# Two 96-point transforms rewritten from split products to plain fp32 strips of 32 columns

## The chip, the cores and the metric

The kernel runs on one core of one Trainium2 chip. The metric is the device time of one execution in microseconds (us); the runs shown are three executions, and their median is the time before.

## What is computed

The reference chains three layers on 24,576 rows of 256 numbers. First a Fourier layer: a real FFT over 3072 positions, a complex 256 by 256 mixing with bias, soft shrinkage by 0.01, and the inverse FFT.

```
X = np.fft.rfft(x, axis=1)
Yr = Xr @ w_r - Xi @ w_i + b_r
Yi = Xr @ w_i + Xi @ w_r + b_i
...
y = np.fft.irfft(Y, n=x.shape[1], axis=1)
```

Then every row picks one of 8 experts by `argmax(x @ w_gate)`; an expert takes at most 768 rows, in order, and applies `relu(h @ w1) @ w2` times the gate's probability. Last comes a second MLP with `h * softmax(h)` and a layer norm between its two products. Experts fill up early, so the kernel transforms only the first three sequences of the batch (`FIRST = 3`) and checks that this was enough.

## The kernel before, in words

The FFT of 3072 positions is done in two steps, 3072 = 96 x 32. Per sequence (a "turn" b = 0, 1, 2):

- **Forward, first step** (`forward`, L949): a 96-point transform of 16 pieces, each 96 x 512 numbers. `prepare` (L332) splits a piece into a high and a low fp32r part (`split`, L280: a copy on ACT, L281, and a subtraction on DVE, L282), and `dft` (L311) makes three fp32r matmuls of them (L314 to L316). Four pieces of sixteen (`WHOLE`; three in the first turn, `WHOLE_0`) skip the split and run as one plain fp32 matmul (L325), which the trace shows as two records. Two pieces share one PSUM tile of 96 x 1024; `leave` (L341) moves it to SBUF on ACT or DVE, `park` (L357) writes it to DRAM (`gdram`, L359), eight writes per turn.
- **Units** (`units`, L985): twelve units u read the data back turned round (`relay`, L366), make 32-point transforms (`stage2`, L380), split them (L383, L384), mix (`mix`, L413), shrink (DVE, L419 to L422) and go back (`inv1`, L430).
- **Tail** (`tail`, L1001): gate logits (L440, four strips of 32 columns beside each other, plain fp32, 384 columns wide), then per piece n four transposes (L459), a split of the transposed piece (L281, L282), the 96-point inverse (`inv2`, L465, again `dft`, `psy`), a move to a `yt` buffer (L473, four of them in turn) and a write to `ydram` (L474). The routing steps `local` and `place` (L504 to L518) stand between the pieces; the marks that follow (L533, L534 on DVE, L536 on POOL, L542 on PE) run in the next turn's units.

After the third turn come the expert blocks (from 338 us to the end), which the change leaves alone.

All loads and writes of these stages are issued by one queue, SP, in program order, and its transfers take eight semaphore lanes in turn: a ninth waits for the first to land. The Tile scheduler sets the order on each engine, so that work without dependencies, like the zeroing of the output (`out`, L909, 512 KB each) and loads of expert weights (L595, L598), is put where it finds room. `load_x` (L296) loads the next sequence in eight parts q: five before the turn ends, q = 5 to 7 inside `forward`, as buffers come free:

```
def x_at(q, roomy):
    if roomy and q >= 3:
        return v3(o_ht + 1024 * (q - 3), 4, D, N1)
    return v3(o_yt + 1024 * (q - 3) if q in (3, 4) else o_xr + 1024 * (q % 5), 4, D, N1)
```

Of the kernel before, what the change touches and what calls it, by code (L numbers as in the profile page):

```python
# [8 lines left out]
F32 = mybir.dt.float32  # L9
# [19 lines left out]
AHEAD = 4  # L29
LEAVE_0 = (1, 3, 5)  # L30
LEAVE = (1, 3, 5)
GATHER = 9


# [9 lines left out]
NCH = 8  # L44
COUNT = 3
SUMS = 7
YT = (13, 15)
LOOK = 4
LOG = 0
WARM = 4  # L50
KEEP = 8
STEPS = (3, 3, 2)
ZEROS = ((0, 0, 0, 0), (2, 2, 2, 2), (2, 2, 2, 2))
WHOLE = (2, 5, 8, 11)
WHOLE_0 = (0, 1, 14)
PERSIST = 16472
EARLY = (0, 1)

# [71 lines left out]
def _body(tc, x, w_r, w_i, b_r, b_i, w_gate, w1, w2, w_in, w_out, g_ln, cap, con, out):  # L130
# [15 lines left out]
    with sp as sb, dp as dr, pp as ps:  # L146
# [49 lines left out]
        o_lt = o_rt  # L196
        ident = v(o_id, 128)
        fraw = v3(o_f, 2, N1, N1)
        o_fs = region(384)
        renew(o_fs)  # L200
        f_h, f_l = R(v3(o_fs, 2, N1, N1)), R(v3(o_fs + 192, 2, N1, N1))
        bias, bias0 = v(o_b, 256), v(o_b0, 256)
        zero = v(o_zero, 128)
        wg = v3(o_wg, 2, 32)
# [21 lines left out]
        g3 = lambda: v3(o_g, N2, D, N1)  # L226
# [38 lines left out]

        def load_f():
            dma(out=fraw, in_=con["c_f"])
            act(f_h, fraw, ACTF.Copy)
            vec.tensor_tensor(f_l, fraw, f_h.bitcast(F32), ALU.subtract)
# [21 lines left out]
        def x_at(q, roomy):  # L291
            if roomy and q >= 3:
                return v3(o_ht + 1024 * (q - 3), 4, D, N1)
            return v3(o_yt + 1024 * (q - 3) if q in (3, 4) else o_xr + 1024 * (q % 5), 4, D, N1)
# [4 lines left out]
        second_half = [o_tt]  # L299

        def piece(n, roomy=False):
            o = (o_hn, second_half[0])[n // 3 % 2] + 1024 * (n % 3)
            if roomy:
                n %= 10
                if n >= 6:
                    o = o_xb[(n - 6) // 2] + 1024 * (n % 2)
                else:
                    o = (o_hn, second_half[0])[n // 3] + 1024 * (n % 3)
            return R(v(o, 512, N1)), R(v(o + 512, 512, N1))
# [8 lines left out]
        def stage1(q, roomy):  # L318
            p = psum("ps1")
            for j in range(2):  # L320
                n = 2 * q + j
                o, (src, parts) = p[:N1, 512 * j : 512 * j + 512], ready.pop(n)
                gone.add(n)
                if parts is None:
                    mm(o, fraw[:, 0], src, start=True, stop=True)  # L325
                else:
                    dft(o, 0, parts, roomy)
            return p

        ready = {}  # L330

        def prepare(n, roomy):  # L332

            src = x_at(n // 2, roomy).rearrange("p a d -> p (a d)")[:, 512 * (n % 2) : 512 * (n % 2) + 512]
            k = None
            if n not in (WHOLE_0 if roomy else WHOLE):
                k = n - sum(i < n for i in (WHOLE_0 if roomy else WHOLE))
                split(*piece(k, roomy), src)
            ready[n] = src, k

        def leave(q, p, on_vec):  # L341
            dst = v(o_g + 1024 * q, 1024, N1)
            if q == 7:
                act(dst[:, 0:512], p[:N1, 0:512], ACTF.Copy)
                vec.tensor_copy(dst[:, 512:1024], p[:N1, 512:1024])
            elif q in on_vec:
                vec.tensor_copy(dst, p[:N1])
            else:
                act(dst, p[:N1], ACTF.Copy)
            park(q)  # L350

        def gd(g):
            return v((o_ga if g % 12 < 6 else o_gb) + 256 * (g % 6), D)

        turn_of = [0]

        def park(q):  # L357

            dma(out=gdram[turn_of[0] % 2][:, 4 * q : 4 * q + 4, :], in_=g3()[:, 4 * q : 4 * q + 4])  # L359
            if q == 7:  # L360
                turn_of[0] += 1

        def relay(g, n=2):
# [88 lines left out]

        turned, summed = [None, None], [None, None]

        def inv2t(n):
# [9 lines left out]
        def inv2(n, yv):  # L465
            if n % 2 == 0:
                summed[0] = psum("psy")
            p = summed[0][:N1, 512 * (n % 2) : 512 * (n % 2) + 512]
            w = dft(p, 1, n)
            if n % 2:  # L470
                apart(w, summed[1])
            yt = v(o_yt + 512 * (n % 4), 512, N1)
            summed[1] = [vec.tensor_copy(yt, p) if n in YT else act(yt, p, ACTF.Copy)]  # L473
            dma(out=yv[:, 2 * n : 2 * n + 2], in_=yt.rearrange("p (a d) -> p a d", d=D))  # L474


        def route(tok_src, chunk_buffers):
# [468 lines left out]
        def in_order(strict):  # L946
            return pinned() if strict else ExitStack()

        def forward(xb, roomy=False, begun=False):  # L949
            if not begun:  # L950
                begin(roomy)
            last = begun_with.pop()
            for q in range(1, 8):
                for n in range(2 * q + 2, min(2 * q + AHEAD + 2, 16)):
                    if n not in ready and n not in gone:
                        with in_order(roomy):
                            prepare(n, roomy)
                if q + 4 < 8 and not roomy:
                    load_x(xb, q + 4)
                p = stage1(q, roomy)  # L960
                if roomy and q == 7:
                    end = [i for i in nc.cur_bb.bb.instructions if i.engine == mybir.EngineType.PE][-1]
                    with tc.issue_after(end):
                        warm(KEEP)
                with in_order(roomy):
                    leave(q - 1, last, LEAVE_0 if roomy else LEAVE)
                last = p
            with in_order(roomy):
                leave(7, last, ())
            gone.clear()  # L970

        begun_with, gone = [], set()

        def begin(roomy=False):

            for n in range(4):
                with in_order(roomy):
                    prepare(n, roomy)
            begun_with.append(stage1(0, roomy))

        def relays():
# [19 lines left out]
        def tail(yv, steps):  # L1001

            logits(0)
            inv2t(0)
            logits(1)
            for n in range(1, LOOK):
                inv2t(n)
            for n in range(16):
                if n + LOOK < 16:
                    inv2t(n + LOOK)  # L1010
                inv2(n, yv)
                if n == LOG:
                    logits2()
                if n % 2 and n // 2 + 1 in steps:
                    for f in steps[n // 2 + 1]:
                        f()

        csum = bias0
# [151 lines left out]
        for b in range(FIRST):  # L1170
# [25 lines left out]
                    if early:  # L1196
                        early.pop(0)()

            def before_last(last=last, steps=steps):
                while steps:  # L1200
                    steps.pop(0)()
                renew(o_hn)
                if last:
                    renew(o_ga)
                    blocks[0].transposes()
                    sums.extend(column_sums())
                    sums.pop(0)()
                else:
                    begin()

            units(middle, before_last)
            while sums:
                sums.pop(0)()
            renew(o_tt)
            if last:
                renew(o_wi2)
                second_half[0] = o_wi2
            if not last:
                forward(x[b + 1], begun=True)
# [23 lines left out]
        renew(o_hn)  # L1243
        marks.append(all_places)
        run_blocks(blocks, side, slot_b, verdict, marks)

# [65 lines left out]
```

## Time and profile before

| what | value |
|---|---|
| median of three runs | 907.37 us (907.3 to 910.01) |
| the profiled execution, own time | 907.39 us |
| its span, first to last instruction | 905.6 us |
| mean granted TensorE clock | 0.976 |
| PE busy | 858.3 us, 95% |
| DVE busy | 660.2 us, 73% |
| ACT busy | 451.3 us, 50% |
| POOL busy | 302.9 us, 33% |

The 1.8 us between span and own time lie around the instructions. PE is TensorE's matmul, PEld its weight load. In the trace the turns' stages lie at: forward 0 from 5.66 us, units 0 from 32.85, forward 1 from 90.23, tail 0 from 110.34 to 136.62, units 1 after it, forward 2 from 201.43, tail 1 from 215.44 to 244.65, units 2 after it, tail 2 from 314.25 to 338.36. The last `inv1` of a turn (L430, 0.9 us, 91.70 to 92.61 in the first) stands inside the next forward.

### The profile page before, as it was taken

The page shows a single profiled execution, that of the slowest core. Times are in us where ns is not written, and L with a number is a line of the kernel's source. Part 1 is how long each engine was busy: PE and PEld are TensorE (multiplying, and loading weights), DVE is VectorE, ACT ScalarE, POOL GpSimd, SP SyncE. Part 2 cuts the span into 40 slices and gives each one's busy share as a digit, 9 for nine tenths or more (in the row PEclk, how much of TensorE's full clock was granted, in tenths as well). Part 3 has the DMA queues.
Part 4 walks back from the last instruction along what each step waited for, and adds up shares of the span by engine and source line. Part 5 has one row for each costly group of instructions (what it writes and reads, how often), then busy time and mean ns, then how long its engine had stood idle before and what let it go on. Part 6 is the DMA issues. An engine that isn't in the chain of part 4 may idle for free.

```text
span 905.6 us, 15391 instructions
## 1 busy us (share of the span) xinstructions
PE 858.3 (95%) x5585; PEld 763.8 (84%) x5585; DVE 660.2 (73%) x1499; ACT 451.3 (50%) x725; POOL 302.9 (33%) x463
## 2 busy tenths in 40 slices
PE   9599899999899998999999999999999999999993
PEld 5599368995699978989899999899889889999983
DVE  6277579777887687777788778678768768777672
ACT  6254464446734372555466456456446446444450
POOL 0000002200031205363754554454544544445343
PEclk9799899999899998999999999999999999999997
DMA  9989869999541133253465463553564463333220
GB/s 284 303 246 301 275 215 266 309 300 297 195 162 36 36 115 102 70 100 71 103 163 114 123 140 82 117 140 91 108 140 87 112 140 86 73 76 65 53 59 28
DMA packets 206699, 130.90 MB, mean 145 GB/s; under 512 B 122406, under 2 KB 190102, under 8 KB 206486
## 3 DMA queue, kind: packets, MB, share of 16 engines
q1 hardware_dynamic: 201910, 117.20, 49.1%
q0 software_dynamic: 4704, 12.63, 4.4%
q8 instruction: 46, 0.75, 0.3%
q14 instruction: 39, 0.32, 0.1%
HBM read 50.37 MB, written 50.33 MB: 111 GB/s over the span
## 4 chain that ended last, share of the span: by engine, by line
PE 72%; DMA 9%; DVE 7%; issue 6%; POOL 2%; ACT 2%; SPq 0%; POOLq 0%; DVEq 0%; ACTq 0%
PE psH L778 13%; PE pso L893 11%; PE psm L413 8%; PE psY L798 5%; PE psY L797 5%; PE psh L823 4%; PE psh L822 4%; PE psY L795 4%; PE psh L825 4%; DMA r<-r 4%; PE psi L430 3%; PE ps L380 3%; PE psr L542 2%; DVE r L282 1%; DMA r<-moe_w_in 1%
## 5 line engine op out<-in xcount | busy, mean ns | idle before, releaser
L778 PE MATMUL psH<-r,r 128*128 128x384 f32 x768 | 147.7, 340 | 0.5 <-DVE r L282 0.5
L778 PEld LDWEIGHTS psH<-r,r 128*128 128x128 f32 x768 | 135.6, 190 | 2.3 <-DVE r L282 0.8
L893 PE MATMUL pso<-r,r 128*128 128x256 f16 (+1 forms) x792 | 134.6, 274 | 0.5 <-DMA r<-r 0.5
L893 PEld LDWEIGHTS <-r 128*128 128x128 f16 x1080 | 102.2, 98 | 18.8 <-issue 6.9
L413 PE MATMUL psm<-r,r 128*128 128x256 f32 x864 | 112.8, 286 | 2.4 <-DVE r L473 2.2
L536 POOL TENSOR_TENSOR r<-r,r 96x192 f32<-96x192 f32 x24 | 19.3, 822 | 278.9 <-DVE r L392 139.3
L413 PEld LDWEIGHTS psm<-r,r 128*128 128x128 f32 x864 | 106.0, 191 | 2.9 <-ACT r L473 1.4
L781 ACT ACTIVATE r<-psH 128x768 fp32r<-128x768 f32 x64 | 52.0, 813 | 105.8 <-PE psH L778 102.7
L839 DVE SCALAR_TENSOR_TENSOR r<-psh,r 128x1024 f32<-128x1024 f32 x48 | 58.8, 1224 | 51.7 <-ACT r L831 51.7
L282 DVE TENSOR_TENSOR r<-r,r 128x512 fp32r<-128x512 f32 (+2 forms) x115 | 81.4, 722 | 14.3 <-ACT r L281 13.9
L798 PE MATMUL psY<-r,r 128*128 128x384 f32 x256 | 86.5, 338 | 4.6 <-DVE r L782 4.3
L797 PE MATMUL psY<-r,r 128*128 128x384 f32 x256 | 85.7, 335 | 0.0
L831 ACT ACTIVATE r<-psh,r 128x1024 f32<-128x1024 f32 x36 | 43.4, 1205 | 82.9 <-DVE r L830 58.9
L893 PE MATMUL pso<-r 128*128 128x256 f16 x360 | 81.0, 273 | 0.0
L896 POOL DMA_INDIRECT out<-r x48 | 56.0, 1167 | 72.1 <-DVE r L895 65.0
L822 PE MATMUL psh<-r,r 128*128 128x512 f32 x192 | 76.5, 399 | 0.0
L823 PE MATMUL psh<-r,r 128*128 128x512 f32 x192 | 75.6, 394 | 0.0
L281 ACT ACTIVATE r<-r 128x512 fp32r<-128x512 f32 (+2 forms) x115 | 71.4, 647 | 7.5 <-DMA r<-x 6.5
L782 DVE SCALAR_TENSOR_TENSOR r<-psH,r 128x768 fp32r<-128x768 f32 x64 | 61.1, 954 | 12.5 <-ACT r L781 11.3
L732 POOL DMA_INDIRECT r<-ydram,r x48 | 50.6, 1053 | 44.1 <-DVE r L758 14.8
L829 DVE TENSOR_REDUCE r<-psh 128x1 f32<-128x1024 f32 x48 | 58.5, 1218 | 8.6 <-PE psh L825 8.6
L869 POOL TENSOR_SCALAR r<-r 128x1 f32<-128x1 f32 x48 | 12.5, 261 | 146.5 <-ACT r L849 115.3
(192 smaller groups left out, 1803.3 us busy)
## 6 DMA issues: line engine op xcount, KB each, us to landing
out<-r SPq DMA_DIRECT2D x48, 512.0 KB
r<-moe_w SPq DMA_DIRECT2D x32, 512.0 KB
r<-x SPq DMA_DIRECT2D x24, 384.0 KB
gdram<-r SPq DMA_DIRECT2D x24, 384.0 KB
r<-gdram SPq DMA_DIRECT2D x36, 256.0 KB
ydram<-r SPq DMA_DIRECT2D x48, 192.0 KB
r<-moe_w_in SPq DMA_DIRECT2D x4, 512.0 KB
r<-moe_w_out SPq DMA_DIRECT2D x4, 512.0 KB
```

Source lines behind the costliest of these rows:

```text
L281: a = act(hi, src, ACTF.Copy)
L282: return a, eng.tensor_tensor(lo, src, hi.bitcast(F32), ALU.subtract)
L413: mm(p3[:, gi], a, b, start=i == 0, stop=i == len(seq) - 1)
L778: mm(p3[:, fi, 0:BLK], a, b, start=i == 0, stop=i == 5)
L782: vec.scalar_tensor_tensor(hl_, p3[:, :, 0:BLK], 0.0, hh.bitcast(F32), ALU.max, ALU.subtract)
L797: mm(y3[:, d, 0:BLK], a, hh[:, fi], start=False, stop=False)
L798: mm(y3[:, d, 0:BLK], a, hl_[:, fi], start=False, stop=f == 7)
L822: mm(o, a, r, start=k == 0, stop=False)
L823: mm(o, a, w, start=False, stop=False)
L829: vec.tensor_reduce(c(0), p, AX.X, ALU.max, negate=True)
L839: vec.scalar_tensor_tensor(t, p, 1.0, e, ALU.mult, ALU.mult, accum_out=c(3))
L893: mm(p[:, 0:D], a, b, start=n == 0, stop=n == 23)
```

## The change

No piece is split any more. A 96-point transform is computed as three strips of 32 output columns in plain fp32, at column positions 0, 32 and 64 of the array; the fourth position takes a third of another piece. So three PSUM banks hold four pieces: twelve banks per transform where there were sixteen pieces, all 128 partitions full. Bank k holds piece `own(k)` = 1, 2, 3, 5, 6, 7, 9, ... and strip k % 3 of piece 0, 4, 8 or 12.

```diff
-        def dft(o, i, n, roomy=False):
-            hi, lo = piece(n, roomy)
-            return [mm(o, f_h[:, i], hi, start=True, stop=False),
-                    mm(o, f_l[:, i], hi, start=False, stop=False),
-                    mm(o, f_h[:, i], lo, start=False, stop=True)]
+        own = lambda k: 4 * (k // 3) + 1 + k % 3
+        def bank(o, i, k, piece):
+            strips = [(m, piece(own(k))) for m in range(3)] + [(k % 3, piece(4 * (k // 3)))]
+            return [mm(o[32 * j : 32 * j + 32], fraw[:, i, 32 * m : 32 * m + 32], src, start=True, stop=True, tile_position=(0, 32 * j))
+                    for j, (m, src) in enumerate(strips)]
...
-            dma(out=gdram[turn_of[0] % 2][:, 4 * q : 4 * q + 4, :], in_=g3()[:, 4 * q : 4 * q + 4])
+            if t % 3 == 0:
+                dma(out=flat(dram[:, r + 2 : r + 6, :]), in_=src[0:N1])
+                dma(out=thirds(0, r), in_=pairs(src[N1:128]))
+            elif t % 3 == 1:
+                dma(out=dram[:, r + 6 : r + 14, :].rearrange("m (j n) d -> m j (n d)", j=2)[:, :, 0 : 2 * D], in_=pairs(src[0:N1]))
+                dma(out=flat(dram[64:96, r : r + 2, :]), in_=src[N1:128, 0:512])
+                dma(out=flat(dram[0:32, r + 8 : r + 10, :]), in_=src[N1:128, 512:1024])
+            else:
+                dma(out=flat(dram[:, r + 12 : r + 16, :]), in_=src[0:N1])
+                dma(out=thirds(32, r + 8), in_=pairs(src[N1:128]))
...
-            turned[1] = split(*piece(n), p)
+            a = piece(n)
+            turned[1] = [vec.tensor_copy(a, p) if n % 2 else act(a, p, ACTF.Copy)]
...
+            dma(out=yv[:, 2 * own(k) : 2 * own(k) + 2], in_=yt[0:N1].rearrange("p (a d) -> p a d", d=D))
+            dma(out=yv[m : m + 32, r : r + 2], in_=yt[N1:128].rearrange("p (a d) -> p a d", d=D))
...
-                begin(roomy)
+                begin(xb, roomy)
...
+            if not roomy:
+                for q in range(5, 8):
+                    load_x(xb, q)
```

`prepare` is gone. A turn's `leave` moves six tiles of 128 x 1024 where it moved eight of 96 x 1024 (LEAVE is now (1, 3)); `park` makes 14 writes for 8, `inv2` 24 for 16. A transposed piece is moved by one copy, on ACT for even n and on DVE for odd n. The parts q = 5 to 7 of the next sequence get buffers of their own (`o_hn`) and are loaded by `begin`, ahead of the first bank. `place` stands after bank 8 of twelve (turns 0, 1) or bank 7 (turn 2), where it stood after piece 11 or 9 of sixteen. Line numbers shift: L298 is the strips' matmul, L333 to L340 the writes, L361 and L394 were L380 and L413, L365 was L384, L521 and L522 were L533 and L534.

The scheduler's order moves with it. The first place is SP around forward 1 (`x` the next sequence, `out` the zeroing, `gdram` the parked tiles). Before:

```order
L909 DMA out<-r_66 1024x1x128 x8
L297 DMA r_66<-x 96x1024 x3
L909 DMA out<-r_66 1024x1x128 x6
L359 DMA gdram_65<-r_69 96x1024
L297 DMA r_66<-x 96x1024
L359 DMA gdram_65<-r_69 96x1024
L297 DMA r_66<-x 96x1024
L359 DMA gdram_65<-r_69 96x1024 x6
```

Now:

```order
L897 DMA out<-r_66 1024x1x128 x8
L288 DMA r_66<-x 96x1024 x2
L288 DMA r_789<-x 96x1024 x3
L897 DMA out<-r_66 1024x1x128 x4
L332 DMA gdram_65<-r_68 96x1024
L333 DMA gdram_65<-r_68 32x2x512
L335 DMA gdram_65<-r_68 96x2x512
L336 DMA gdram_65<-r_68 32x512
```

The last two parts of x stood behind six zeroing writes and between parked tiles; all of x now stands ahead of four zeroing writes.

The second place is DVE after `place` in tail 0, where units 1 begin (L384 and L365 make the low part that the first mix needs, L473 and L459 move the last results). Before:

```order
L518 CAST r_66<-r_66 96x32
L533 TENSOR_TENSOR r_1222<-r_66 96x512
L473 COPY r_66<-psy 96x512
L384 TENSOR_TENSOR r_71<-ps_1170,r_71 128x4x128
L389 CAST r_71<-r_71 128x256
```

Now:

```order
L506 CAST r_66<-r_66 96x32
L521 TENSOR_TENSOR r_1173<-r_66 96x512
L522 TENSOR_TENSOR r_1173<-r_66 96x192
L521 TENSOR_TENSOR r_66<-r_66 96x512
L522 TENSOR_TENSOR r_66<-r_66 96x192
L522 TENSOR_TENSOR r_1173<-r_66 96x192
L365 TENSOR_TENSOR r_70<-ps_1121,r_70 128x4x128
L370 CAST r_70<-r_70 128x256
L522 TENSOR_TENSOR r_66<-r_66 96x192
L373 TENSOR_SCALAR r_70<-r_70 128x4
```

Five mark steps now stand ahead of L365 where one stood ahead of L384; the third L522 reuses a buffer that POOL has to have read. In turn 1 three stand there.

## Rows read from the trace of the kernel before

**Rows 1.** The page's part 4: the chain that ended last, by engine.
```profile
PE 72%; DMA 9%; DVE 7%; issue 6%; POOL 2%; ACT 2%; SPq 0%; POOLq 0%; DVEq 0%; ACTq 0%
```
**Rows 2.** Waits of PE: line waited for, us in total, times, longest us.
```profile
PE ps L380 <- DMA r<-gdram: 9.7, 1, 9.7
...
PE psr L542 <- POOL r L536: 3.7, 1, 3.7
PE ps L314 <- ACT r L281: 3.4, 2, 1.8
...
PE psy L314 <- ACT r L473: 1.8, 1, 1.8
```
**Rows 3.** Windows by stage: length, busy us by engine, granted clock, DMA share, GB/s.
```profile
90.23:136.62 46.39, 41.66 (x214) 25.07 (x213) 29.20 (x55) 26.22 (x46) 0.00 (x0) 0.93 0.79 247
136.62:147.66 11.04, 9.07 (x73) 8.51 (x71) 9.66 (x27) 5.29 (x12) 2.59 (x4) 1.00 0.89 265
201.43:244.65 43.22, 41.33 (x213) 26.57 (x212) 32.01 (x60) 30.26 (x54) 0.00 (x0) 0.92 0.82 261
244.65:256.54 11.89, 9.08 (x73) 8.54 (x72) 10.88 (x29) 5.16 (x12) 3.12 (x4) 1.00 0.77 255
314.25:338.36 24.11, 24.11 (x162) 16.83 (x162) 19.27 (x44) 16.44 (x32) 0.00 (x0) 1.00 0.33 99
338.36:346.03 7.67, 3.99 (x21) 3.68 (x20) 5.53 (x14) 1.93 (x4) 3.40 (x4) 0.85 0.41 126
```
**Rows 4.** The same view, five microseconds each, in tail 1.
```profile
225.00:230.00 5.00, 5.00 (x34) 3.93 (x32) 4.77 (x12) 5.00 (x11) 0.00 (x0) 1.00 1.00 344
...
235.00:240.00 5.00, 5.00 (x16) 3.44 (x16) 2.31 (x5) 2.94 (x6) 0.00 (x0) 0.50 0.87 273
```
**Rows 5.** Timeline of PE in tail 2: start, us, line, operation, count.
```profile
314.25 1.50 PE L440 MATMUL psl<-r 128*32 128x384 f32 x16
315.68 0.64 PE L459 MATMUL pst<-r 128*96 128x128 f32 x4
316.25 0.83 PE L440 MATMUL psl<-r 128*32 128x384 f32 x2
...
319.00 0.97 PE L459 MATMUL pst<-r 128*96 128x128 f32 x7
319.81 0.60 PE L444 MATMUL psl<-r 128*96 128x128 f32 x4
```
**Rows 6.** Timeline of PE in forward 1.
```profile
97.34 1.02 PE L325 MATMUL ps<-r 96*96 96x512 f32 x2
97.79 0.79 PE L314 MATMUL ps<-r,r 96*96 96x512 f32 x1
98.42 0.39 PE L315 MATMUL ps<-r,r 96*96 96x512 f32 x1
98.65 0.39 PE L316 MATMUL ps<-r,r 96*96 96x512 f32 x1
```
**Rows 7.** Groups by line and form, the strips' weight loads: busy us, mean ns.
```profile
L440 PEld LDWEIGHTS psl<-r 128*32 128x32 f32 x96 | 3.3, 115 | 6.3 <-issue 5.8 <-PE ps L316 0.4
```
**Rows 8.** The same view, the low part of transposed pieces on DVE.
```profile
L282 DVE TENSOR_TENSOR r<-pst,r 96x512 fp32r<-96x512 f32 x48 | 32.2, 681 | 11.4 <-ACT r L281 11.3
```
**Rows 9.** Timeline of SP: issues at the start, and around forward 1.
```profile
15.48 8.18 SPq L359 DMA_DIRECT2D gdram<-r  x8
...
95.94 1.11 SPq L297 DMA_DIRECT2D r<-x  x1
```
**Rows 10.** Timeline of DVE after place in tail 0.
```profile
133.54 0.16 DVE L506 TENSOR_TENSOR r<-pso,r 96x8 f32<-96x8 f32 x1 [0.80 <-PE pso L505]
...
137.88 0.18 DVE L518 CAST r<-r 96x32 f32<-96x32 int32 x1
...
143.67 0.65 DVE L534 TENSOR_TENSOR r<-r 96x192 f32<-96x192 bf16 x1 [0.87 <-POOL r L536]
```
**Rows 11.** Windows, three microseconds of the start, columns as in rows 3.
```profile
18.00:21.00 3.00, 3.00 (x13) 1.92 (x12) 3.00 (x5) 2.54 (x4) 0.00 (x0) 1.00 1.04 414
```

More of the change, by code (lines that the diff above doesn't have):

```diff
@@ L28 @@
 FIRST = 3
-AHEAD = 4
-LEAVE_0 = (1, 3, 5)
-LEAVE = (1, 3, 5)
+LEAVE_0 = (1, 3)
+LEAVE = (1, 3)
 GATHER = 9
@@ L46 @@
 SUMS = 7
-YT = (13, 15)
+YT = (9, 11)
 LOOK = 4
@@ L53 @@
 ZEROS = ((0, 0, 0, 0), (2, 2, 2, 2), (2, 2, 2, 2))
-WHOLE = (2, 5, 8, 11)
-WHOLE_0 = (0, 1, 14)
 PERSIST = 16472
@@ L293, in x_at @@
                 return v3(o_ht + 1024 * (q - 3), 4, D, N1)
-            return v3(o_yt + 1024 * (q - 3) if q in (3, 4) else o_xr + 1024 * (q % 5), 4, D, N1)
+            return v3((o_xr + 1024 * q, o_yt + 1024 * (q - 3), o_hn + 1024 * (q - 5))[(q >= 3) + (q >= 5)], 4, D, N1)
         def load_x(xb, q, roomy=False):
             dma(out=x_at(q, roomy), in_=xb.rearrange("(a n) d -> a n d", n=N2)[:, 4 * q : 4 * q + 4])
[L299 to L309, printed above, removed]
@@ L319, in stage1 @@
+        def stage1(t, roomy):
             p = psum("ps1")
+            x_of = lambda n: x_at(n // 2, roomy).rearrange("p a d -> p (a d)")[:, 512 * (n % 2) : 512 * (n % 2) + 512]
             for j in range(2):
[L321 to L327, printed above, removed]
@@ L328, in stage1 @@
-            return p
[L330 to L347, printed above, removed]
-            else:
-                act(dst, p[:N1], ACTF.Copy)
-            park(q)
+                bank(p[:, 512 * j : 512 * j + 512], 0, 2 * t + j, x_of)
@@ L352, in gd, with leave @@
+            return p
+        def leave(t, p, on_vec):
+            dst = v(o_g + 1024 * t, 1024)
+            if t == 5:
+                act(dst[:, 0:512], p[:, 0:512], ACTF.Copy)
+                vec.tensor_copy(dst[:, 512:1024], p[:, 512:1024])
+            elif t in on_vec:
+                vec.tensor_copy(dst, p)
+            else:
+                act(dst, p, ACTF.Copy)
+            park(t)
         def gd(g):
@@ L355, in _body, with park @@
         turn_of = [0]
-        def park(q):
-            dma(out=gdram[turn_of[0] % 2][:, 4 * q : 4 * q + 4, :], in_=g3()[:, 4 * q : 4 * q + 4])
-            if q == 7:
+        def park(t):
+            dram, src = gdram[turn_of[0] % 2], v(o_g + 1024 * t, 1024)
+            r = 16 * (t // 3)
+            pairs = lambda a: a.rearrange("p (b c) -> p b c", b=2)
+            thirds = lambda a, b: dram[a : a + 64, b : b + 2, :].rearrange("(b m) n d -> m b (n d)", b=2)
+            flat = lambda a: a.rearrange("m n d -> m (n d)")
+            if t % 3 == 0:
[8 more added lines that the diff above has]
+                dma(out=thirds(32, r + 8), in_=pairs(src[N1:128]))
+            if t == 5:
                 turn_of[0] += 1
@@ L453, in _body @@
         turned, summed = [None, None], [None, None]
+        second_half = [o_tt]
+        piece = lambda n: v((o_hn, second_half[0])[n // 6 % 2] + 512 * (n % 6), 512, N1)
         def inv2t(n):
@@ L462, in inv2t, with inv2 @@
                 apart(w, turned[1])
-            turned[1] = split(*piece(n), p)
-        def inv2(n, yv):
-            if n % 2 == 0:
+            a = piece(n)
+            turned[1] = [vec.tensor_copy(a, p) if n % 2 else act(a, p, ACTF.Copy)]
+        def inv2(k, yv):
+            if k % 2 == 0:
                 summed[0] = psum("psy")
-            p = summed[0][:N1, 512 * (n % 2) : 512 * (n % 2) + 512]
-            w = dft(p, 1, n)
-            if n % 2:
+            p = summed[0][:, 512 * (k % 2) : 512 * (k % 2) + 512]
+            w = bank(p, 1, k, piece)
+            if k % 2:
                 apart(w, summed[1])
-            yt = v(o_yt + 512 * (n % 4), 512, N1)
-            summed[1] = [vec.tensor_copy(yt, p) if n in YT else act(yt, p, ACTF.Copy)]
-            dma(out=yv[:, 2 * n : 2 * n + 2], in_=yt.rearrange("p (a d) -> p a d", d=D))
+            yt = v(o_yt + 512 * (k % 4), 512)
+            summed[1] = [vec.tensor_copy(yt, p) if k in YT else act(yt, p, ACTF.Copy)]
+            m, r = 32 * (k % 3), 8 * (k // 3)
+            dma(out=yv[:, 2 * own(k) : 2 * own(k) + 2], in_=yt[0:N1].rearrange("p (a d) -> p a d", d=D))
+            dma(out=yv[m : m + 32, r : r + 2], in_=yt[N1:128].rearrange("p (a d) -> p a d", d=D))
         def route(tok_src, chunk_buffers):
@@ L950, in forward @@
             if not begun:
-                begin(roomy)
+                begin(xb, roomy)
             last = begun_with.pop()
[L953 to L961, printed above, removed]
+            for t in range(1, 6):
+                p = stage1(t, roomy)
+                if roomy and t == 5:
                     end = [i for i in nc.cur_bb.bb.instructions if i.engine == mybir.EngineType.PE][-1]
@@ L965, in forward, with begin @@
                 with in_order(roomy):
-                    leave(q - 1, last, LEAVE_0 if roomy else LEAVE)
+                    leave(t - 1, last, LEAVE_0 if roomy else LEAVE)
                 last = p
             with in_order(roomy):
[L969 to L978, printed above, removed]
+                leave(5, last, ())
+        begun_with = []
+        def begin(xb, roomy=False):
+            if not roomy:
+                for q in range(5, 8):
+                    load_x(xb, q)
             begun_with.append(stage1(0, roomy))
@@ L1005, in tail @@
             logits(1)
-            for n in range(1, LOOK):
+            for n in range(1, LOOK + 1):
                 inv2t(n)
[L1008 to L1012, printed above, removed]
+            for k in range(12):
+                for n in range(own(k - 1) + LOOK + 1 if k else LOOK + 1, min(own(k) + LOOK, 15) + 1):
+                    inv2t(n)
+                inv2(k, yv)
+                if k == LOG:
                     logits2()
-                if n % 2 and n // 2 + 1 in steps:
-                    for f in steps[n // 2 + 1]:
+                for q in range(8 * k // 12 + 1, 8 * (k + 1) // 12 + 1):
+                    for f in steps.get(q, ()):
                         f()
@@ L1197, in middle, with before_last @@
                         early.pop(0)()
-            def before_last(last=last, steps=steps):
+            def before_last(b=b, last=last, steps=steps):
                 while steps:
@@ L1208, in before_last @@
                 else:
-                    begin()
+                    begin(x[b + 1])
             units(middle, before_last)
@@ L1215, in _body @@
             if last:
-                renew(o_wi2)
+                renew(o_wi2, o_hn)
                 second_half[0] = o_wi2
@@ L1241, in verdict @@
             vec.tensor_copy(fl[:, 1:2].bitcast(I32), fl[:, 0:1])
-        renew(o_hn)
+        renew(o_hn, o_wi2)
         marks.append(all_places)
```

7 lines of the change are left out of this document (removed).

## The prediction

> **What bounds the kernel now.** I read the chain of waits first: PE holds 72% of it [rows 1], so a change counts where it takes PE time or where PE waits. The list of PE's waits is short: besides the one at the start, 9.7 us until the data of turn 0 are back from DRAM, it names the marks of tail 2, 3.7 us, the splits of forward 1, 3.4 us, and an eviction in tail 1, 1.8 us [rows 2]. Three of these lie in the stages that the change rewrites. So I cut the program into stages [rows 3]. Tail 2 is PE's own: 24.11 of 24.11 us busy at full clock. Forward 1 with tail 0 takes 46.39 us and forward 2 with tail 1 43.22 us, with the clock at 0.93 and 0.92. What holds tail 1 is seen close up: ACT is busy 5.00 of 5 us and DVE 4.77, then PE waits, and ten microseconds on the clock is at 0.50, 1.2 GHz [rows 4]. The splits are what fills ACT and DVE there, so their removal can pay twice.
>
> **The price of a bank.** The trace has both kinds of matmul at 512 columns. L325 and one L314 start 1.08 us ahead of L315, and an fp32r matmul takes 0.23, so a whole fp32 piece takes 0.85 [rows 6]. How four strips share the array is not seen at 512 columns, but at 384: eight strip matmuls, 16 records in four positions, are followed by the next work after 1.43 us [rows 5]. At full clock a record of two passes over 384 columns is 0.32 us; one after the other they would need 5.1, four deep they need 1.28. So the positions run beside each other and 0.15 is left for the change back. I take 0.85 per bank, as long as one whole piece. The other end, no overlap, is 3.4. A change of form costs on the way in as well: four transposes between strips take 0.57 [rows 5], seven ahead of other transposes 0.81, that is 0.46 for four; so 0.11 in and 0.15 out, 0.26 a visit.
>
> **The change, part by part.**
>
> Forward on PE: before 12 x 3 x 0.23 + 4 x 0.85 = 11.7 us, now 12 x 0.85 + 2 x 0.26 = 10.7.
>
> Tail on PE: 48 x 0.23 = 11.0 becomes 12 x 0.85 = 10.2 plus about ten visits between transposes, 2.6. A tail without waits thus grows by 1.8, from 24.1 to 25.9. In tail 2, where PE never waited, this is a loss: **+1.8**.
>
> Forward and tail of turns 0 and 1: if no wait is left, 10.7 + 0.9 (the inv1 inside) + 25.9 = 37.5 us. Against 46.39 that is **-8.9**, against 43.22 **-5.7**. What must cover PE: the splits are replaced by one copy per piece, so of 48 DVE subtractions at 0.68 [rows 8] half remain as copies; evictions fall from sixteen to twelve. That leaves 28 copies and evictions of some 0.7 us for two engines in 19 us. And x must come in time. Before, q = 6 was issued at 95.94 [rows 9], after PE had begun at 90.2, and q = 7 behind the next parked tile; now all eight parts stand ahead of the last zeroing writes, some ten microseconds earlier, while the last bank needs them at about 100. In tail 1, eight splits of expert weights also leave for units 2, where DVE has room: I price them at **+0.5** for small delays.
>
> The seam after tail 0: units 1 now start behind more of the marks. From L506 to L518 it took 4.5 us with one split of 0.6 between [rows 10], so 3.9. Then come four mark steps, 1.8, and the third L522 waits for POOL, whose two products held L534 up before too [rows 10]; L365 ends some 8.1 us after the place matmul. PE, with three banks and two transforms to do, is through after 5.1 and stands for 3 us, and a little more at L373. The stage took 11.04 us with 9.07 busy [rows 3]; I expect 1.7 more. After a wait of 1.8 us in tail 1 the clock fell for about 6 us [rows 2, 4]; a wait of 3 is likely to do it, and half of that time is lost, partly under DVE: 2.5. Together **+4.2**. In turn 1 L365 stands behind three marks, and PE stands 1.5 us where the stage had 2.8 idle: **-0.5**. In turn 2 the marks keep their distance from the tail's end: **+0.3** on the 7.67 us [rows 3].
>
> The start: forward 0 loses its splits and ends some two microseconds sooner, but the DMA share there is 1.04 [rows 11], so all DMA engines are busy, and the writes wait for it. The same 3 MB now go in 14 writes. By bytes nothing changes, and one load of constants has moved behind the first relays: **-1**. By count it would be 14 x 1.1 us where 8 took 8.2 to issue [rows 9], 7 more. I take the bytes, since the eight writes moved at the DMA's pace, and keep both ends. In turns 1 and 2 the writes, and the 24 to ydram, have a tail of 25 us to land in.
>
> Sum: -1.0 - 8.9 - 5.7 + 1.8 + 4.2 - 0.5 + 0.3 + 0.5 = -9.3. From the profiled execution's 907.4, which is the median of the runs too, this gives **898 us**.
>
> **Rivals.**
>
> *Strips that do not hide their weights* (slower). A strip needs its own weight load, 115 ns at 32 columns [rows 7], twice per bank and position. If it had to wait until that position's matmul is over, a bank would take 0.85 + 0.23, and 72 banks 16.6 us more: 915 us. It decides from 0.13 us per bank on, where 72 banks eat the 9.3. Against it: 16 records in 1.43 us leave no room for four such loads per position [rows 5], but those strips were shorter and read two weights only.
> The Trainium skill speaks for a like result: "TensorE: Matmul & The Clock Gate", section "Measured speedup vs the span model", gives 3.07 times for four 512-column tiles beside each other in rows, and 2.38 for three in columns. By 3.07 a bank would be an estimated 4 x 0.85 / 3.07 = 1.11 us and the kernel 917 us; by the trace's row the gain is 5.1 / 1.43 = 3.6 even with the change back, so the measurement is the better guide here.
>
> *The starts take it back* (no change). The writes cost by count, the first relays come 6 us later instead of 1 sooner, and PE stands at L380 for 16 us: 905 us. The DMA's pace speaks against it, the eight lanes and the eight writes of 64 or 128 KB for it.
>
> *x comes late again* (faster, less). SP is in order, and q = 3 to 7 wait for buffers behind the weight staging of turn 0. If they land after 100 us, the 3.4 us of waits [rows 2] and 3 of low clock in forward 1 stay: 904 us.
>
> That the strips are not made can be left aside: the order shows four per bank.
>
> **How the numbers follow.** The forecast has 0.72, x late 0.08, the starts 0.10, the weights 0.08, and 0.02 is left for what I don't see. A measurement of this kernel tells about 0.3% from no change, 2.7 us. Faster than 904.7 is then 0.80, within 0.11, slower 0.09. If the clock does not fall at the seam, 895 comes out; if the fuller engines had cost more than I counted, 889. The range goes from there past x late and the starts: 889 to 906.
>
> **What would show it.** Right: a record of L298 every 107 ns or so in a forward, forwards of 11 to 12 us, no wait for x in forward 1, clock near 1 in both stages, tail 2 longer by 1 to 2 us, a new wait at L394 for L365 after tail 0, perhaps with 1.2 GHz behind it. Wrong: a bank of 1 us or more in a run of banks without transposes, a wait at L361 of more than 10 us at the start, or the old waits in forward 1 and tail 1.

## The result and the profile after

The changed kernel takes **896.36 us**, median of four runs (894.88 to 897.53), the kernel before 908.0 (907.3 to 910.01); the ratio is 0.9867, 95% interval 0.9842 to 0.9892. Forecast were 898 us and a range of 889 to 906. The profiled execution took 897.53 us with a span of 895.9, 9.7 less than the span before. First the chain by engine and the waits of PE that are longest, as in [rows 1, 2]:

```profile
PE 85%; DMA 7%; DVE 4%; issue 1%; SPq 1%; ACT 1%; POOL 0%; DVEq 0%; POOLq 0%; ACTq 0%
```
```profile
PE ps L361 <- DMA r<-gdram: 10.8, 1, 10.8
PE psY L786 <- DVE r L770: 4.6, 4, 1.8
PE psm L394 <- DVE r L365: 4.5, 2, 3.1
PE psr L530 <- POOL r L524: 3.3, 1, 3.3
```

The waits of forward 1 and of tail 1 are gone, the wait at the start has grown by 1.1 us, and L394 for L365 is new. The same stages as in [rows 3], by windows (length, busy by engine, granted clock, DMA share, GB/s):

```profile
89.91:126.97 37.06, 37.06 (x311) 15.10 (x310) 17.66 (x36) 14.14 (x23) 0.00 (x0) 1.00 0.79 244
126.97:141.20 14.23, 10.75 (x77) 10.18 (x73) 9.75 (x26) 5.04 (x11) 2.36 (x4) 0.88 0.26 80
195.11:232.18 37.07, 37.07 (x312) 15.11 (x311) 17.86 (x36) 14.13 (x23) 0.00 (x0) 1.00 0.76 241
232.18:242.97 10.79, 9.06 (x76) 8.64 (x73) 9.17 (x25) 4.94 (x11) 1.96 (x4) 1.00 0.49 150
300.42:325.89 25.47, 25.47 (x209) 11.32 (x208) 15.19 (x35) 10.73 (x20) 0.00 (x0) 1.00 0.31 94
325.89:333.29 7.40, 4.09 (x25) 3.77 (x21) 5.15 (x13) 1.77 (x3) 2.80 (x4) 0.82 0.38 115
```

PE is now busy in every microsecond of the first, third and fifth stage, at full clock. All stages, by their first instructions on PE (a tail begins here with its first logits, before at 106.97 and 213.57, where the last few matmuls of the forward still follow):

| stage | before, us | after, us | difference | forecast |
|---|---|---|---|---|
| start, to the first L361 | 32.85 | 32.61 | -0.2 | -1.0 |
| units 0 | 57.38 | 57.30 | -0.1 | 0 |
| forward 1 + tail 0 | 16.74 + 29.65 | 11.54 + 25.52 | -9.3 | -8.9 |
| seam 0 | 11.04 | 14.23 | +3.2 | +4.2 |
| units 1 | 53.77 | 53.91 | +0.1 | 0 |
| forward 2 + tail 1 | 12.14 + 31.08 | 11.55 + 25.52 | -6.2 | -5.7 |
| seam 1 | 11.89 | 10.79 | -1.1 | -0.5 |
| units 2 | 57.71 | 57.45 | -0.3 | +0.5 |
| tail 2 | 24.11 | 25.47 | +1.4 | +1.8 |
| seam 2 | 7.67 | 7.40 | -0.3 | +0.3 |
| expert blocks from there | 559.6 | 562.6 | +3.0 | 0 |

The price of a bank, from the timeline of PE in forward 1 (compare [rows 6]):

```profile
97.16 0.60 PE L298 MATMUL ps<-r,r 96*32 96x512 f32 x3
97.18 0.59 PE L298 MATMUL ps<-r 96*32 96x512 f32 x1
97.59 0.60 PE L298 MATMUL ps<-r,r 96*32 96x512 f32 x3
...
98.88 2.76 PE L298 MATMUL ps<-r,r 96*32 96x512 f32 x24
```

Four records start within 0.02 us of each other, and the next four 0.43 us later: eight records, a bank, per 0.86 us, one record per 107 ns. The four strips together take what one whole piece takes, so their weight loads cost nothing that shows. The Trainium skill, "TensorE: Matmul & The Clock Gate", section "Measured speedup vs the span model", has 3.07 times for four tiles in rows and 2.38 for three in columns, and no row for four in columns; this run of banks is a factor of 4 (4 x 0.85 / 0.86), and the measurement decides.

In seam 0 the new wait is the one foreseen, with low clock behind it:

```profile
126.97 2.05 PE L361 MATMUL ps<-r,r 128*128 128x128 f32 x16
132.13 2.41 PE L394 MATMUL psm<-r,r 128*128 128x256 f32 x9 [3.11 <-DVE r L365]
134.34 1.86 PE L361 MATMUL ps<-r,r 128*128 128x128 f32 x8
```

Eight records of L361 take 1.86 us there and 1.06 at full clock.

**Where the 9.3 us of turn 0 came from.** In the trace of before, PE waited twice for ACT in forward 1. At the first of the two waits ACT itself stood for x; before the second, ACT stood for PE's L316, with the copy for PE behind an eviction in its own queue. Two rows of ACT's timeline, and two windows:

```profile
101.67 1.15 ACT L281 ACTIVATE r<-r 96x512 fp32r<-96x512 f32 x2 [1.57 <-DMA r<-x]
...
104.28 1.02 ACT L349 ACTIVATE r<-ps 96x1024 f32<-96x1024 f32 x1 [1.45 <-PE ps L316]
```
```profile
100.00:106.97 6.97, 3.56 (x11) 1.21 (x9) 3.54 (x5) 3.31 (x6) 0.00 (x0) 0.85 1.00 347
106.97:112.00 5.03, 5.03 (x21) 1.67 (x20) 0.86 (x2) 0.59 (x1) 0.00 (x0) 0.53 0.31 108
```

PE's gaps in forward 1 were 3.4 us [rows 2], and the clock then stood at 0.53, close to 1.2 GHz, for the first five microseconds of tail 0: 2.4 us of work lost (5.03 x 0.47), and up to 1.0 in the window before. Tail 0 was idle for another 1.3. That is up to 8.1 of the 9.3. In tail 1, 31.08 us at a mean of 0.89, the same two losses were 1.9 us idle and 3.4 of clock, 5.3 of the 6.2.

The trace of before has two stages that show what the splits do to PE when nothing else is amiss. Forward 2 has the same splits as forward 1, and PE never waits in it. Tail 0 and tail 2 give ACT and DVE nearly the same work, and in tail 2 PE never waits [rows 3]; tail 1 gives them more, with eight splits of expert weights. The windows of tail 0, forward 2 and tail 1 of before:

```profile
106.97:136.62 29.65, 28.32 (x164) 18.04 (x164) 18.84 (x41) 16.27 (x31) 0.00 (x0) 0.92 0.63 197
201.43:213.57 12.14, 12.14 (x51) 7.11 (x50) 9.59 (x14) 9.40 (x15) 0.00 (x0) 1.00 0.95 292
213.57:244.65 31.08, 29.19 (x163) 19.46 (x163) 22.42 (x47) 20.86 (x40) 0.00 (x0) 0.89 0.77 249
```

So the splits by themselves did not make PE wait in a forward or in a tail like tail 0. In tail 1 their load, with the expert splits on top, may have.

**Where 3 us went again.** Windows of ten microseconds at the start of the expert blocks, of before and then of after:

```profile
338.36:348.36 10.00, 6.32 (x28) 6.01 (x27) 7.52 (x19) 1.93 (x4) 4.13 (x6) 0.77 0.42 132
348.36:358.36 10.00, 10.00 (x64) 10.00 (x64) 7.00 (x15) 3.70 (x7) 3.76 (x7) 0.89 0.40 93
```
```profile
325.89:335.89 10.00, 6.69 (x32) 6.37 (x29) 7.33 (x18) 1.77 (x3) 3.81 (x6) 0.73 0.41 133
335.89:345.89 10.00, 10.00 (x66) 10.00 (x66) 8.23 (x16) 4.20 (x8) 4.10 (x9) 0.92 0.39 94
...
495.89:505.89 10.00, 8.97 (x49) 8.34 (x50) 6.65 (x19) 4.93 (x8) 4.43 (x8) 0.83 0.20 59
```

Both kernels lose up to some three microseconds to low clock right there (10 x 0.27 and 10 x 0.08 for the change, which counts PE's idle time too), behind a wait of 3.7 and 3.3 us at L530 for POOL (L542 in [rows 2]). After has a second place at 496 us, 1.7 lost, behind one of the four waits at L786, 1.8 us. Before has none there. From the first to the last record of L766 before takes 520.8 us and after 523.6. Seven experiments whose clock also falls there show 518.7 to 521.2 over the same records, so some of these 3 us look like one execution's chance.

### The profile page after: what moved, and what is told of

Its sections match the earlier page's. It is cut to its first block, busy times and chain, and to the rows that moved or that the text cites. A ratio compares the mean times of both kernels' runs of the same rounds, so it can differ in the third digit from the quotient of the medians.

```text
span 895.9 us, 15838 instructions
## 1 busy us (share of the span) xinstructions
PE 853.4 (95%) x5884; PEld 736.1 (82%) x5884; DVE 621.7 (69%) x1434; ACT 410.7 (46%) x648; POOL 300.6 (34%) x463
## 4 chain that ended last, share of the span: by engine, by line
PE 85%; DMA 7%; DVE 4%; issue 1%; SPq 1%; ACT 1%; POOL 0%; DVEq 0%; POOLq 0%; ACTq 0%
PE psH L766 14%; PE pso L881 12%; PE psm L394 11%; PE psY L786 5%; PE psh L811 4%; PE psY L785 4%; PE psh L810 4%; PE psh L813 4%; DMA r<-r 4%; PE psY L783 4%; PE ps L361 4%; PE psi L411 4%; PE psy L298 4%; PE pst L443 3%; PE psr L530 2%; PE ps L298 2%
## 5 line engine op out<-in xcount | busy, mean ns | idle before, releaser
L766 PE MATMUL psH<-r,r 128*128 128x384 f32 x768 | 149.0, 342 | 0.6 <-DVE r L273 0.6
L766 PEld LDWEIGHTS psH<-r,r 128*128 128x128 f32 x768 | 136.9, 192 | 3.1 <-ACT r L459 0.8
L394 PE MATMUL psm<-r,r 128*128 128x256 f32 x864 | 114.2, 288 | 4.9 <-DVE r L365 4.5
L394 PEld LDWEIGHTS psm<-r,r 128*128 128x128 f32 x864 | 107.0, 193 | 5.7 <-DVE r L365 4.8
L524 POOL TENSOR_TENSOR r<-r,r 96x192 f32<-96x192 f32 x24 | 17.3, 738 | 265.7 <-DVE r L522 133.2
L786 PE MATMUL psY<-r,r 128*128 128x384 f32 x256 | 86.9, 339 | 4.7 <-DVE r L770 4.6
L785 PE MATMUL psY<-r,r 128*128 128x384 f32 x256 | 86.0, 336 | 0.0
L273 DVE TENSOR_TENSOR r<-r,r 128x512 fp32r<-128x512 f32 (+1 forms) x78 | 57.4, 743 | 0.8 <-ACT r L272 0.7
L783 PE MATMUL psY<-r,r 128*128 128x384 f32 x256 | 56.8, 343 | 0.0
```

The source lines that it names most:

```text
L394: mm(p3[:, gi], a, b, start=i == 0, stop=i == len(seq) - 1)
L766: mm(p3[:, fi, 0:BLK], a, b, start=i == 0, stop=i == 5)
L783: mm(y3[:, d, 0:BLK], b, hh[:, fi], start=f == 0, stop=False)
L785: mm(y3[:, d, 0:BLK], a, hh[:, fi], start=False, stop=False)
L786: mm(y3[:, d, 0:BLK], a, hl_[:, fi], start=False, stop=f == 7)
```

## The experiments

My theory: the strips cost PE about what the split form did; the gain is that PE no longer waits for ACT and DVE, which the splits filled, and that x comes early. Rivals: PE's own time is the gain; late x alone was the loss. The first two kernels take the strips away again, in the tail and then everywhere.

**e1, tails of whole pieces; e2, no strips at all.** Sixteen fp32 matmuls of 96 columns where there were 12 banks, sixteen evictions:

```diff
-            w = bank(p, 1, k, piece)
+            w = [mm(p, fraw[:, 1], piece(k), start=True, stop=True)]
```
and in e2 also, with eight parked tiles as before:
```diff
-                bank(p[:, 512 * j : 512 * j + 512], 0, 2 * t + j, x_of)
+                mm(p[:N1, 512 * j : 512 * j + 512], fraw[:, 0], x_of(2 * t + j), start=True, stop=True)
```

> The forwards keep their strips; in the tails each of the 16 pieces is one whole fp32 matmul again (no split, evictions as in the change's form, 16 instead of 12). My terms: 16 x 0.85 = 13.6 us where strips take 12 x 0.85 + about ten visits of 0.26 = 12.8, and tail 2 of the change measured 25.5, so a tail of about 26.3 to 26.7: plus 1 in each of three tails, 898 to 901 us. Rival, a visit between transposes costs more than I counted (the strips lose in the tail): tails of 25.5 or less, 896 or below. Rival, the evictions are short of time (16 against 12): a tail above 27.5 with waits of PE for psy or pst, above 902.

> No strip anywhere: 16 whole fp32 pieces in forward and tail, no splits, x early, eight parked tiles as in the kernel before. If most of the gain is the splits' absence and x's early load, and the strips only pay for the fp32 passes, this stands at: forward 13.6 instead of 11.5 us (turns 1 and 2, plus 2 each; forward 0 lies under the DMA), tails plus 1 each: 901 to 905 us, still below the kernel before. Rival, the strips' PE time is the gain: as slow as before or slower, 908 or more, since PE then does 27.2 us per turn where it did 22.7 with splits.

e1: 892.38 us, ratio 0.9829 (0.9808 to 0.985). Its tails take 26.5, 26.5 and 26.0 us, about what my terms said, 0.5 to 1.0 more than strips; yet it ends 4 us earlier than the change. It has no long wait in seam 0 (10.7 us; seam 1 takes 12.4, 1.6 more than in the change), and at the start of the blocks PE waits less and keeps its clock:

```profile
PE psr L528 <- POOL r L522: 2.3, 1, 2.3
```
```profile
327.64:337.64 10.00, 7.71 (x49) 7.15 (x48) 7.86 (x16) 4.21 (x7) 4.03 (x8) 1.00 0.60 156
```

So the expected total was wrong and the tails right: what lies behind the tails weighed more than the strips in them. e2: 899.17 us, 0.9897 (0.9871 to 0.9922), below my 901 by the same clock. Its forwards take 14.72 us, 3.2 more than with strips (I said 2), its tails 26.0 to 26.7. Forward 1 with tail 0 is 41.1 us and forward 2 with tail 1 41.4: against [rows 3] the missing waits are worth 5.3 and 1.9 us, net of PE's longer work on whole fp32 pieces, and the strips take off another 4.0 and 4.3. Both halves count; neither rival stands alone.

**e3, the splits' load back in tails 0 and 1.**

```diff
-            turned[1] = [vec.tensor_copy(a, p) if n % 2 else act(a, p, ACTF.Copy)]
+                h = v(o_g + 6144 + 512 * (n % 4), 512, N1)
+                turned[1] = [act(h, p, ACTF.Copy), vec.tensor_tensor(a, p, h, ALU.max)]
```

> The change, with the splits' load put back on ACT and DVE in the tails of turns 0 and 1: each piece is first copied by ACT and then written by a DVE operation of two inputs that waits for that copy, as the low part did. PE's work is untouched. My theory (the splits filled both engines and PE waited for them): these two tails grow from 25.5 to 28 to 30 us, with waits of PE for DVE or ACT in them and perhaps 1.2 GHz behind, 902 to 906 us. Rival (the splits were hidden, PE's own time was the gain): 896 to 898 and tails of 25.5 to 26.

893.92 us, 0.9843 (0.9816 to 0.987), not slower than the change. The tails do grow, to 27.45 us, but PE waits for nobody in them and the clock is 1.00. Its timeline shows what grew:

```profile
111.25 1.04 PE L298 MATMUL psy<-r,r 96*32 96x512 f32 x2
112.22 0.64 PE L443 MATMUL pst<-r 128*96 128x128 f32 x4
112.80 1.06 PE L298 MATMUL psy<-r,r 96*32 96x512 f32 x6
```

A bank is cut in two by other work, twice per tail; one strip by itself (two records) holds PE for 0.97 us, as long as four. So the load makes PE wait nowhere in these tails and reaches it only through the order that the scheduler makes. The total hides the 3.9 us by which two tails grew: seam 0 takes 10.78 us here, with a wait of 0.9 at L394 where the change has 3.1. My theory finds no support in the tails; it is not refuted for the kernel before, whose split form left ACT and DVE less time (a tail of 24.1 us on PE alone, against 25.5 in the change).

**e4, x late.** Parts 5 to 7 of x go into the buffers of parts 0 to 2 again, loaded inside the forward.

```diff
-            return v3((o_xr + 1024 * q, o_yt + 1024 * (q - 3), o_hn + 1024 * (q - 5))[(q >= 3) + (q >= 5)], 4, D, N1)
+            return v3(o_yt + 1024 * (q - 3) if q in (3, 4) else o_xr + 1024 * (q % 5), 4, D, N1)
```

> The change, with x of parts 5 to 7 loaded into the two kernels' common buffers again, which are free only when the forward has used parts 0 to 2, so that these loads stand among the parked tiles in SP's queue. If the early loads carried the gain of the forwards (my rival priced late x at 6 us): waits of PE for x or in forward 1 and 2 of 3 us and more, 901 to 904. If the splits alone held the forwards up: waits under 1 us, 896 to 898.

912.9 us, 1.0051 (1.0024 to 1.0077): slower than the kernel before. SP's timeline around forward 1, the waits of PE from 85 to 125 us, and the windows of forward 1 and tail 0:

```profile
82.59 12.48 SPq L897 DMA_DIRECT2D out<-r  x7
95.17 1.57 SPq L332 DMA_DIRECT2D gdram<-r  x1
96.79 0.44 SPq L333 DMA_DIRECT2D gdram<-r  x1
97.33 1.04 SPq L288 DMA_DIRECT2D r<-x  x1
```
```profile
PE ps L298 <- DMA r<-x: 5.8, 2, 5.5
```
```profile
89.75:111.77 22.02, 16.17 (x105) 4.36 (x108) 3.50 (x4) 4.27 (x5) 0.00 (x0) 0.76 0.96 291
111.77:138.81 27.04, 27.04 (x211) 11.56 (x203) 14.19 (x32) 10.69 (x19) 0.00 (x0) 0.94 0.65 198
```

The load of part 5 is issued at 97.33, behind seven zeroing writes and a parked tile; 5.8 us of waits and a mean clock of 0.76 make the forward 22.0 us instead of 11.5, the second one 20.2. The early place of x is no side issue of the change: without it everything is lost, 16.5 us. It puts the loads in another place of SP's queue than the kernel before had them, so it is no measure of what was lost there. The opposite run, the kernel before with x early, was not made; forward 2 of before, where ACT stood only 0.49 us for x, is the nearest to it.

**e5 and e9, all of the old load.** e5 is e3 (with two spare buffers) and eight more pairs of ACT copy and DVE subtraction, unused, among the banks of tail 1, where before had eight splits of expert weights; e9 is the same on the tails of whole pieces, so with four evictions more.

```diff
+                if len(spare) == 1 and 2 <= k < 10:
+                    with pinned():
+                        split(R(v(o_g + 7168, 512)), R(v(o_g + 7680, 512)), v(o_mix, 512))
```

> The change, with in tails 0 and 1 each piece copied by ACT and then written by DVE after that copy (as in the third experiment), and in tail 1 eight more pairs of an ACT copy and a DVE subtraction of 128 x 512 among the banks, unused, where the kernel before had eight splits of expert weights. If it was the sum of both loads that made PE wait in tail 1 of before (2.8 us of waits and 1.2 GHz behind): tail 1 of 28.5 us or more, with waits of PE, against 27.5 without the eight pairs; tail 0 stays at 27.4. If the engines' load does not reach PE at all: tail 1 at 27.5.

> The tails as whole fp32 pieces (16 evictions of 96 partitions instead of 12 of 128) with all of the copies of the fifth experiment: ACT and DVE then carry in tail 1 what they carried in the kernel before, 37 ACT operations, with fp32 in place of the three fp32r passes on PE. If load and the four evictions more together made PE wait: tail 1 of 29 us or more with waits of PE for psy or pst, against 26.5 for the whole pieces alone, and 1.2 GHz behind. If not: 26.5 to 27.5 in both tails, and the waits of before come from something else in its order.

e5: 895.96 us in one run; tail 0 takes 25.7 us without a wait of PE, tail 1 26.3 with 0.8 of waits. In this kernel no bank is cut apart, so tail 0 is shorter than in e3. e9: 900.64 us in one run, tails of 28.0 and 27.0 us, idle for 1.0 in each, mostly here:

```profile
PE psy L459 <- DVE r L450: 1.1, 2, 0.7
```

In all these tails the clock stays at 1.00. But the load does not vanish: part of it runs on past the tail. Within tail 1 ACT has 33 operations in e5 (with four evictions fewer) and 36 in e9, where before had 40. Seam 1 takes 12.86 us in e5, where the change takes 10.79, and 14.43 in e9, where e1 takes 12.41. The windows of tail 1 and seam 1 in e9:

```profile
206.49:233.44 26.95, 25.99 (x144) 13.77 (x137) 20.45 (x42) 18.21 (x36) 0.00 (x0) 1.00 0.66 207
233.44:247.87 14.43, 10.31 (x75) 9.05 (x75) 12.88 (x34) 9.83 (x21) 2.75 (x4) 0.94 0.95 297
```

So here the load costs PE at most 1.0 us of waits in a tail and about 2 us in the seam behind tail 1. The expert splits alone, which stand in tail 1 of e2 too, made PE wait 0.02 us there. None of this tells what it cost before, where PE asked for a piece sooner. For tail 0 the trace of before names the larger part of the loss, 2.4 of 3.7 us: the low clock behind the waits of forward 1. For tail 1 ACT's timeline of before shows:

```profile
228.67 1.68 ACT L281 ACTIVATE r<-r 128x512 fp32r<-128x512 f32 x3
...
232.62 0.59 ACT L281 ACTIVATE r<-pst 96x512 fp32r<-96x512 f32 x1 [1.29 <-PE pst L459]
233.11 0.58 ACT L473 ACTIVATE r<-psy 96x512 f32<-96x512 f32 x1
```

Three expert splits of 1.7 us stand in a row, then ACT waits 1.3 us for transposes, and PE's eviction L473 stands behind them in the same queue. That points to the order of the queue as much as to its load; no run here tells the two apart, and it stays argued.

**e6, marks held back.** The marks of units 1 and 2 may no longer overtake the units' work.

```diff
                 if b > 0 and marks:
-                    marks.pop(0)()
+                    with pinned():
+                        marks.pop(0)()
```

> The change, with each step of the marks in units 1 and 2 held on DVE behind the last DVE and ACT instruction that stands ahead of it in the program, so that L365 of the first units goes first. If the three microseconds at L394 and the low clock behind them come from the marks ahead of L365: seam 0 falls from 14.2 to 10 to 11 us, seam 1 from 10.8 to about 9.5, 890 to 893 us. Rival (L365 is late for another reason, or the marks come back as waits in the units): seam 0 stays over 13 or units 1 and 2 grow by as much, 895 to 898.

892.07 us, 0.9837 (0.9796 to 0.9879). Seam 0 takes 9.86 us, seam 1 9.68; L394 waits 0.52 where it waited 3.11:

```profile
129.21 1.50 PE L394 MATMUL psm<-r,r 128*128 128x256 f32 x9 [0.52 <-DVE r L365]
```

That is 4.4 and 1.1 us less, so the cause of the new wait is shown. Units 1 and 2 give back 1.4 and 1.6: L530 now waits for POOL 5.8 us in three places, 2.5 more.

**e7, banks in pairs.** The transposes that two banks need are done ahead of both.

```diff
-                for n in range(own(k - 1) + LOOK + 1 if k else LOOK + 1, min(own(k) + LOOK, 15) + 1):
-                    inv2t(n)
+                if k % 2 == 0:
+                    for n in range(done + 1, min(own(k + 1) + LOOK, 15) + 1):
+                        inv2t(n)
+                        done = n
```

> The change, with the tail's banks taken two at a time wherever a bank holds two halves of one PSUM tile, so that four changes between transposes and strips fall away per tail. By my 0.26 us a visit tail 2 goes from 25.5 to 24.4 and all three tails give 3 us: 893. Rival (the transposes in longer rows run out of PSUM or of copies): waits of PE for L448, tails of 25.5 or more, 896 to 900.

891.51 us, 0.9842 (0.9799 to 0.9884), an interval that holds the change's ratio. The tails take 24.70, 24.70 and 24.89 us: 0.82 and 0.58 less for four visits, 0.15 to 0.2 a visit where I had 0.26. Tail 2 is still longer than before's 24.11.

**e8, the start of the blocks.** The place arithmetic of turn 2 comes one step earlier, and its marks take the free buffer first.

```diff
-ROUTE = ((-2, -6), (-2, -6), (-2, -5))
+ROUTE = ((-2, -6), (-2, -6), (-2, -4))
-            local, place, marks = route(con["c_tok"][b], (o_hn + 1536, o_rt))
+            local, place, marks = route(con["c_tok"][b], (o_rt, o_hn + 1536) if last else (o_hn + 1536, o_rt))
```

> The change, with the place arithmetic of turn 2 one eighth of the tail earlier, and its marks' two buffers taken in the other order, so that the first marks need not wait for the last piece. The trace shows PE waiting 3.3 us at L530 for L524 at the start of the expert blocks, and the granted clock at 0.73 and 0.92 in the 20 us that begin there; where the tails are whole pieces the wait is 2.3 and the clock stays at 1.00. If the wait brings the clock down: no wait above 1.5 us there, the clock at 1, and 4 to 5 us less, 891 to 892. Rival (the clock falls there for another reason): only the wait goes, 893 to 894.

889.12 us, 0.9795 (0.9762 to 0.9828). PE waits for nobody in the first 20 us of the blocks, and its clock stays:

```profile
328.08:338.08 10.00, 10.00 (x70) 10.00 (x67) 9.80 (x18) 3.63 (x6) 3.82 (x6) 1.00 0.69 178
338.08:348.08 10.00, 10.00 (x70) 9.89 (x69) 8.63 (x18) 3.33 (x6) 7.25 (x8) 1.00 0.43 134
```

From the first to the last record of L766 it takes 516.4 us, 7.2 less than the change in its profiled run, more than the wait (3.3) alone.

**e10, 28 writes at the start.** The 14 writes of turn 0's tiles are cut into halves of their columns.

```diff
+                elif len(in_.shape) == 2:
+                    dma(out=out[:, 0:c], in_=in_[:, 0:c])
+                    dma(out=out[:, c : 2 * c], in_=in_[:, c : 2 * c])
```

> The change, with each of the 14 writes of parked tiles of turn 0 cut into two of half the columns: the same bytes in 28 writes. If the start goes by bytes: the first relay is issued at 29 to 30 us and L361 starts at 32 to 34, as in the change; the time is the change's, 895 to 898. If it goes by count (0.75 us from one write's issue to the next in the change): ten microseconds more at L361, 905 or above.

899.28 us, 0.9905 (0.9889 to 0.992): between the two. SP's timeline of the change, then of this kernel:

```profile
16.20 0.32 SPq L332 DMA_DIRECT2D gdram<-r  x1
...
29.49 1.40 SPq L347 DMA_DIRECT2D r<-gdram  x3
```
```profile
16.46 0.32 SPq L337 DMA_DIRECT2D gdram<-r  x1
...
32.63 1.40 SPq L359 DMA_DIRECT2D r<-gdram  x3
```

The first relay is 3.1 us later and L361 starts at 36.91 instead of 32.61, 0.2 to 0.3 us for each write more. Halving also halved the runs of memory that a write is made of, so number and size of pieces aren't told apart.

**e11 and e12, the three gains together.** e11 is e6, e7 and e8 in one kernel; e12 holds only the first three steps of the marks. The cut shows e12 against e11:

```diff
-                    with in_order(True):
+                    with in_order(u < 3):
                         marks.pop(0)()
```

> Pinned marks, paired banks and the earlier place of turn 2 together. Alone they gave 4, 5 and 7 us against the change. If they work in different places (seams 0 and 1, the tails, the start of the blocks) they add up: 880 to 884. If part of each was chance in the blocks: 885 to 889.

> As the one before, but only the first three steps of the marks are held behind the units' work. The units lost 1.4 and 1.6 us where all were held, in waits at L530 for L524. If holding the first three is enough for the seam: seam 0 at 10 to 11 us, units 1 at 54 and units 2 at 57.5, and 2 us less than with all held. If not: seam 0 over 12.

e11 takes **883.91 us**, ratio 0.9736 (0.9721 to 0.9751), e12 884.77, 0.9746 (0.9728 to 0.9764): the same, and the best of the study. Singly the three gave 4.3, 4.9 and 7.2 us, together 12.4 of that sum of 16.4. In e11 the seams take 9.84 and 9.67 us, the tails 24.7 to 24.9, and the blocks start at full clock. Units 1 and 2 stay at 55.3 and 59.0; e12 does not help them (55.6 and 59.2). No run has e6 and e8 with the whole pieces of e1, so that strips pay in the tail of this kernel rests on the length of the tails alone (24.7 to 24.9 against 26.0 to 26.5).

## Why the prediction was right

The total came out 1.6 us below the forecast, and its two large terms and the one large loss have the right size. That the total is so close is partly luck: up to the expert blocks the profiled execution is 12.7 us ahead where 9.3 were forecast, and the blocks, which were not in the sum, gave 3.0 back. The reason given for the two large terms was wrong in part.

- **The bank** at 0.85 us: 0.86 in a run of banks. The rival of weights that don't hide needed 0.13 more per bank; it is out.
- **Forwards** 10.7 plus 0.9 for the inverse transforms inside: 11.54 and 11.55. **Tails** 25.9: 25.5. A visit costs 0.15 to 0.2 us rather than 0.26, which covers the 0.4.
- **The waits of turns 0 and 1**: size right (-9.3 and -6.2 for -8.9 and -5.7), cause wrong for turn 0 and open for turn 1. The step that failed is the 3.4 us that it books as "the splits of forward 1": at the first of these waits ACT itself stood for x (1.57 us), the second followed from ACT's order, and forward 2 has the same splits without a wait. The low clock behind these waits, 2.4 us, was most of what tail 0 had lost; the rest cannot be the splits' load alone, since tail 2 of before has that load and no wait. For tail 1 the step "The splits are what fills ACT and DVE there, so their removal can pay twice." reads the load rightly, but that the load was the cause is not shown: with most of it put back (e5, e9) PE waited 0.8 and 1.0 us in the tail at full clock, where before had idle 1.9 and the low clock besides, and PE's own work was longer in these runs. I read the engine that PE waited for and did not ask what that engine waited for.
- **x late again** was priced at 6 us; e4, with the loads at a worse place than before had them, measured 16.5. "x must come in time" was the step that carried more than I gave it.
- **Seam 0**: +4.2 forecast, +3.2 measured, wait and low clock as described; e6 shows the cause. Seam 1 went -1.1 instead of -0.5.
- **The start**: -1 forecast, -0.2 measured. The writes cost neither by bytes alone (nothing) nor 1.1 us each: e10 gives 0.2 to 0.3 us, so six writes more would be 1.3 to 1.8 us, enough to take up what the shorter forward gave; the first relay went from 28.39 to 29.49.
- **Units 2** at +0.5 for the moved expert splits: -0.3, nothing.
- **The expert blocks** were not in the sum: +3.0 in the profiled execution, part of it low clock behind one more wait.

## What to carry to other kernels

When the list of waits names an engine, look at that engine's own wait before pricing its load: here ACT stood for a DMA at the first wait of forward 1. Look too for a stage with the same load and no wait, which tells whether the load is the cause; here there were two in the trace of before. Price a wait of PE with the low clock in the windows behind it, since that was as large as the wait itself, and where PE waits at a seam ask which instructions stand in front of the one it waits for, because holding those back, or starting them earlier, gave more here than the strips did in the tail. Four strips beside each other pay where bank follows bank and none is cut apart; one strip alone costs as much as four.

## What the runs showed of the hardware that was not expected

Which wait of PE brings the clock down can't be told from its length. Mean granted clock over the seam, or over the ten microseconds that begin with the blocks:

| place | wait, us | clock |
|---|---|---|
| seam 0, L365 | 3.1 | 0.88 in the change, in e8 and e10; 1.00 in e7 |
| blocks, L530 | 3.3 | 0.73 in the change, 0.74 to 0.86 in e3, e4, e5, e6, e7, e10 |
| blocks, L530 | 2.3 | 0.73 in e9; 1.00 in e1 and e2 |
| seam 1, L394 | 1.6 | 0.86 in e1 |
| seam 1, L394 | 1.4 | 1.00 in the change |
| blocks, L786 at 495 us | 1.8 | 0.83 in the change, over ten microseconds |

The same program text stands around seam 0 in the change and in e10; e7 differs only in the tail ahead. What else decides is open. A fall cost up to three microseconds, about what the wait itself did.

In the tails a strip alone held PE for 0.97 us up to the next transposes (e3), and four hold it for 1.00. More and smaller writes of the same bytes, while the DMA engines were busy at the start, delayed what came behind them by 0.2 to 0.3 us each (e10).
